# Key blocks copied out of PSUM once and masked from SBUF by VectorE, in a two-layer spectral and attention kernel

## The chip, the cores and the metric

The kernel runs on one core of a Trainium2 chip. The metric is the device time of one execution in microseconds (us). Engine names in the profile: PE is TensorE's matmuls, PEld its weight loads, DVE is VectorE, ACT is ScalarE, POOL is GpSimd, SP is SyncE, which here only issues DMAs.

## What is computed

The input x is 2048 rows of 512 bf16 values. Two different sublayers alternate, twice each:

```
x = x + A(layernorm(x)); x = x + B(layernorm(x))      # layer one
x = x + A(layernorm(x)); x = x + B(layernorm(x))      # layer two
A: irfft2(rfft2(x) * (w_r + 1j*w_i))                  # a spectral filter over rows and columns
B: q = x@wq in 32 heads of 16; k = x@wk, v = x@wv     # one key and one value head for all
   softmax(q k^T / 4) v, heads joined, @ wo
```

## The kernel before, in words

The 2048 rows are held as four blocks t of four 128-row tiles r. A program in Python (class Plan, lines 116 to 578) writes down the order of every instruction ahead of time. Each piece of work is a Task with an engine (or a choice of engines), an assumed duration, its dependencies and a place in an order of preference; Plan keeps a clock for each engine and always issues what can start first. So a change of one task's durations or dependencies, or of one of Plan's constants, changes the order of everything that is issued behind it.

Sublayer A (add_front, add_middle, add_back, lines 732 to 876) is done as matrix products with tables. Its back end goes block by block, t = 0 to 3: inverse transforms (inv, L1197, copied out at L1257), additions on VectorE (radix_v, L67 to L77), the product y that gives the new rows (y_mm, L1237), for blocks 1 to 3 the addition to x (add_x, L1248), row statistics (bn, L1028 and L1029), the reciprocal deviation on ScalarE (rstd, L1040 and L1041), a small shift (L1045), the normalisation (apply, L1052), the transposes (tr_n, L1254, copied out at L1257), and then keys, queries and values of the block.

The keys of a block are one product k_mm (L1271) into one PSUM bank. The weight wk8 repeats the 16 key columns eight times, so the 128 partitions hold eight copies of the key block, and two layouts are made of it: KA keeps the even copies and zeroes the odd, KB the reverse. The masks are the two columns of `part` (zeros and ones, one per partition). Before the change both layouts are written straight from the PSUM bank, by two tasks that may each go to ScalarE (L1277) or VectorE (L1279); the bank is released when both are done. Values are one product v_mm (L1283) and four small copies (L1291 and L1293). Queries are qt_mm (L1297).

Sublayer B's scores (L1313) go in one of two ways. A pair of 512-wide scores goes into one of two double banks sa and is turned by ScalarE with one exponential (L1318). A single score goes into one of four banks b and is turned by VectorE with a linear map to 16-bit integers (L1325), whose bits read as bf16 approximate the exponential; groups of up to four of these get two more versions with a constant added to the integers, on GpSimd (L1329) or VectorE (L1331), and the three are averaged in the products with the values (PV, L1335). Plan deals the scores out to whichever engine is free.

While the back end still runs, only ScalarE takes scores, and only for the blocks whose keys and values are there: that stretch is called the ramp here. When the values of the last block are there (v_got, line 858), VectorE takes scores too. Within the ramp, a background matmul task may be put ahead of scores that ScalarE is about to need by as much as SLIP_RAMP; afterwards SLIP = 100 holds (line 406). The fill method (line 454) adds matmuls of zeros (L1010, L1014) where TensorE would be slack. When a block of attention rows is done, its results are transposed and scaled on VectorE (L1342 to L1362), projected (proj, L1366), added to x, and for layer two the front end's work on them is mixed into layer one's attention.

SBUF tiles of the tag xnt (six buffers) hold the normalised rows that are transposed.

Of the kernel before, what the change touches and what calls it, by code (L numbers as in the profile page):

```python
# [8 lines left out]
ACT = mybir.ActivationFunctionType  # L9
ALU = mybir.AluOpType  # L10
P = 128
BF = mybir.dt.bfloat16
# [86 lines left out]
class Task:  # L99
# [5 lines left out]
    def __init__(self, eng, dur, deps, fn, take=None, give=(), then=None, prio=-1, order=0, lazy=0.0, gap=0.0, parts=1, port=False, lock=False, cols=None):  # L105
        self.ways = {eng: dur} if isinstance(eng, str) else dict(zip(eng, dur))
        self.eng, self.deps, self.fn = next(iter(self.ways)), deps, fn
        self.dur = self.ways[self.eng]
        self.take, self.give, self.then = take, give, then
        self.port, self.lock = port, lock  # L110
        self.cols = self.dur * 512.0 / 220.0 if cols is None else cols
        self.prio, self.order, self.lazy, self.gap, self.parts, self.step = prio, order, lazy, gap, parts, 0
        self.end = self.slot = None


class Plan:
# [25 lines left out]
    LATE = 0.0  # L142
    GAP = 0.0
    SLIP = 100.0
    SLIP_RAMP = 1200.0
    PATIENT = 1000.0
    URGE = 150.0
    TURN = 7000.0
# [231 lines left out]
    def pe_next(self):  # L380
# [21 lines left out]
        for b in self.bg_next("PE"):  # L402
            k, n = b[3], 99
            late = T - max(b[5], k.born)
            if kinds and c[0][0] <= b[0] + k.dur + self.PE_SW:
                room = max(limit, c[0][0]) + (self.SLIP if self.at.dve_on else self.SLIP_RAMP) - b[0] - self.PE_SW
                fit = int(room / (k.dur / k.parts)) if room > 0 else 0
# [270 lines left out]
class Layer:  # L678
# [15 lines left out]
    def __init__(self, plan, em, first, last):  # L694
        self.plan, self.em, self.first, self.last = plan, em, first, last
        self.next = None
        self.at = Attn(plan, em, self)
        self.rs = {}
        self.Pk, self.G, self.FT, self.W, self.Dz, self.IT, self.UT, self.V, self.sb, self.xn, self.xt = ({} for _ in range(11))
        self.mm1_done = {}  # L700
        self.g_done = {}
        self.stat = {}
        self.gate = []
        self.two, self.direct = ((x[0] if first else x[1]) for x in (self.TWO, self.DIRECT))
        self.sd_of = {}
# [95 lines left out]
    def add_back(self):  # L801
        p, em, at = self.plan, self.em, self.at
        left = [T]
        for t in range(T):
            o = 20 + 10 * t
            cs = []
            for b in range(2):
                es = []
                for j in range(2):
                    if t == 0 and not self.direct:  # L810
                        m = p.add("PE", 440.0, [self.mid[2 * j]], lambda k, t=t, b=b, j=j: em.inv(self, t, b, j, k.slot, (0,)),
                                  take="b", order=o)
                        n = p.add("PE", 440.0, [m, self.mid[2 * j + 1]],
                                  lambda k, t=t, b=b, j=j, m=m: em.inv(self, t, b, j, m.slot, (1,)), order=o)
                    elif t == 0:
                        m = p.add("PE", 880.0, [self.fil[2 * j]], lambda k, b=b, j=j: em.inv0(self, b, j, k.slot, 0),
                                  take="b", order=o)
                        n = p.add("PE", 880.0, [m, self.fil[2 * j + 1]],
                                  lambda k, b=b, j=j, m=m: em.inv0(self, b, j, m.slot, 1), order=o)
                    else:  # L820
# [3 lines left out]
                                    give=(m,), order=o))  # L824
# [3 lines left out]
            for j in range(0, R, w):  # L828
                key, ks = ("b", t, j), []
                for i, r in enumerate(range(j, j + w)):  # L830
# [3 lines left out]
                              order=o + 1)  # L834
                    if put:
                        c = p.add("ACT", 482.0, [y], lambda k, t=t, r=r, y=y: em.put_x(t, r, y.slot), order=o + 1)
# [7 lines left out]
                                    order=o + 2))  # L844
# [4 lines left out]
                for a in range(j, j + w, 2):  # L849
# [3 lines left out]
                                    lambda k, t=t, a=a, x=x: em.trn_evac(self, t, a, x.slot, k.eng), give=(x,), order=o + 4))  # L853

            def k_got(k, t, i):
                at.k_ready[(t, i)] = k.end + p.LAT[k.eng]
# [7 lines left out]

            m = p.add("PE", 870.0, te, lambda k, s, t=t: em.k_mm(self, t, k.slot, s), parts=4, take="b", order=o + 5)
            last = []
            for i in range(2):
                last.append(p.add(*self.flex(t, 586.0, 667.0), [m], lambda k, t=t, i=i, m=m: em.k_evac(t, i, m.slot, k.eng), order=o + 5))
            p.both(*last, m, lambda k, t=t, last=last: k_got(k, t, last.index(k)))
            if t == 0:  # L870
                at.add_qt((0, 0), te, o + 5)
            m = p.add("PE", 800.0, te, lambda k, s, t=t: em.v_mm(self, t, k.slot, s), parts=4, cols=256.0, take="b", order=o + 6)
# [52 lines left out]
class Emit:  # L925
# [345 lines left out]
        self.nc.tensor.matmul(self.ps(slot), lhsT=self.wk8[:, c, :], rhs=self.xTc(L.at, t, c), start=(c == 0), stop=(c == NC - 1),  # L1271
                              skip_group_check=True)

    def k_evac(self, t, i, slot, eng):
        out, part = (self.KA, self.KB)[i][:, 512 * t:512 * t + 512], self.part[:, i:i + 1]
        if eng == "ACT":
            self.nc.scalar.activation(out=out, in_=self.ps(slot), func=ACT.Identity, scale=part)  # L1277
        else:
            self.nc.vector.tensor_scalar(out=out, in0=self.ps(slot), scalar1=part, scalar2=None, op0=ALU.mult)  # L1279

    def v_mm(self, L, t, slot, r):
        for c in range(NC):
# [174 lines left out]
```

## Time and profile before

| what | us |
|---|---|
| median of 3 runs | 1343.77 (1343.35 to 1345.37) |
| the profiled execution | 1343.35 |
| its span, first to last instruction | 1341.6 |
| VectorE busy, ScalarE busy | 1291.2, 1225.7 |
| GpSimd busy | 849.7 |
| layer one's ramp ends (first L1325) | 110.73 |
| layer two's ramp ends (first L1325 of layer two) | 776.12 |

The granted TensorE clock is 1.00 throughout. A row of the timeline gives the start, the duration, engine, line, operation, what is written from what, the count, and in brackets the idle time of the engine just before and what ended it. Durations include an overlap with the next instruction of the same engine, so distances between starts are what an instruction costs its engine; two evacuations with 0.75 us each start 0.66 us apart, for example. Times run from the span's start.

### The profile page before, as it was taken

The page shows a single profiled execution, that of the slowest core. Times are in us where ns is not written, and L with a number is a line of the kernel's source. Part 1 is how long each engine was busy: PE and PEld are TensorE (multiplying, and loading weights), DVE is VectorE, ACT ScalarE, POOL GpSimd, SP SyncE. Part 2 cuts the span into 40 slices and gives each one's busy share as a digit, 9 for nine tenths or more (in the row PEclk, how much of TensorE's full clock was granted, in tenths as well). Part 3 has the DMA queues.
Part 4 walks back from the last instruction along what each step waited for, and adds up shares of the span by engine and source line. Part 5 has one row for each costly group of instructions (what it writes and reads, how often), then busy time and mean ns, then how long its engine had stood idle before and what let it go on. Part 6 is the DMA issues. An engine that isn't in the chain of part 4 may idle for free. (4 is left out here: it accounts for less than half of the span.)

```text
span 1341.6 us, 31639 instructions
## 1 busy us (share of the span) xinstructions
PE 1310.9 (98%) x13046; PEld 428.0 (32%) x13046; DVE 1291.2 (96%) x2317; ACT 1225.7 (91%) x1390; POOL 849.7 (63%) x831
## 2 busy tenths in 40 slices
PE   9999999999999999999999999999999999999998
PEld 4642222222222222222246422222222222322222
DVE  6998999999999999999969999999999999999998
ACT  6478999999999999899954889999999999998996
POOL 0004777767776777667720068777777777876775
PEclk9999999999999999999999999999999999999999
DMA  9100000010001000100051000000000000000000
GB/s 292 41 1 1 2 1 2 2 33 1 2 2 33 1 2 2 32 2 2 1 165 41 1 1 1 2 2 6 13 2 2 6 13 2 2 1 17 1 1 17
DMA packets 29041, 25.16 MB, mean 19 GB/s; under 512 B 8672, under 2 KB 27616, under 8 KB 28896
## 3 DMA queue, kind: packets, MB, share of 16 engines
q1 hardware_dynamic: 28608, 22.58, 5.7%
q8 instruction: 102, 1.67, 0.5%
q10 hardware_dynamic: 288, 0.56, 0.1%
q14 instruction: 43, 0.35, 0.1%
HBM read 17.89 MB, written 3.67 MB: 16 GB/s over the span
## 5 line engine op out<-in xcount | busy, mean ns | idle before, releaser
L1313 PEld LDWEIGHTS <-KB 32*128 32x128 bf16 x2048 | 83.9, 91 | 224.0 <-issue 218.5
L1313 PEld LDWEIGHTS <-KA 32*128 32x128 bf16 x2048 | 82.3, 91 | 226.0 <-issue 217.8
L1335 PEld LDWEIGHTS <-vs_108 128*32 128x32 bf16 x2464 | 96.3, 94 | 111.3 <-issue 107.7
L1335 PEld LDWEIGHTS <-vs_109 128*32 128x32 bf16 x1632 | 96.3, 94 | 71.4 <-issue 69.0
L1335 PEld LDWEIGHTS <-vs_111 128*32 128x32 bf16 x1632 | 72.1, 94 | 72.7 <-issue 67.6
L1335 PEld LDWEIGHTS <-vs_110 128*32 128x32 bf16 x1632 | 70.0, 94 | 75.4 <-issue 71.9
L1329 POOL INT64_ADD w_1384<-w_1383 x1 | 1.0, 1041 | 110.5 <-DVE w_1383 L1325 110.5
L1329 POOL INT64_ADD w_10948<-w_10947 x1 | 1.0, 1039 | 97.7 <-DVE w_10947 L1325 97.7
L1318 ACT ACTIVATE e_2_86<-sa_65 128x1024 bf16<-128x1024 f32 x47 | 51.1, 1088 | 4.5 <-PE sa_64 L1313 4.0
L1318 ACT ACTIVATE e_12_96<-sa_65 128x1024 bf16<-128x1024 f32 x47 | 51.1, 1087 | 4.5 <-PE sa_64 L1313 4.1
L1318 ACT ACTIVATE e_5_89<-sa_65 128x1024 bf16<-128x1024 f32 x49 | 53.2, 1086 | 1.8 <-PE sa_64 L1313 1.0
L1318 ACT ACTIVATE e_7_91<-sa_64 128x1024 bf16<-128x1024 f32 x50 | 54.7, 1095 | 0.0
L1318 ACT ACTIVATE e_9_93<-sa_65 128x1024 bf16<-128x1024 f32 x49 | 53.2, 1086 | 1.6 <-PE sa_64 L1313 0.8
L1318 ACT ACTIVATE e_0_84<-sa_65 128x1024 bf16<-128x1024 f32 x47 | 51.7, 1101 | 3.2 <-PE sa_64 L1313 3.1
L1318 ACT ACTIVATE e_6_90<-sa_65 128x1024 bf16<-128x1024 f32 x49 | 53.1, 1083 | 1.5 <-PE sa_64 L1313 1.0
L1318 ACT ACTIVATE e_1_85<-sa_64 128x1024 bf16<-128x1024 f32 x50 | 54.2, 1083 | 0.0
L1318 ACT ACTIVATE e_3_87<-sa_65 128x1024 bf16<-128x1024 f32 x47 | 51.4, 1093 | 2.3 <-PE sa_64 L1313 2.0
L1318 ACT ACTIVATE e_11_95<-sa_65 128x1024 bf16<-128x1024 f32 x47 | 51.4, 1093 | 2.2 <-PE sa_64 L1313 1.9
L1318 ACT ACTIVATE e_4_88<-sa_65 128x1024 bf16<-128x1024 f32 x49 | 53.0, 1081 | 0.1
L1318 ACT ACTIVATE e_12_96<-sa_64 128x1024 bf16<-128x1024 f32 x48 | 52.7, 1099 | 0.2 <-PE sa_64 L1313 0.2
L1318 ACT ACTIVATE e_10_94<-sa_64 128x1024 bf16<-128x1024 f32 x49 | 52.5, 1072 | 0.1
L1318 ACT ACTIVATE e_3_87<-sa_64 128x1024 bf16<-128x1024 f32 x48 | 52.2, 1086 | 0.1
(4003 smaller groups left out, 6246.9 us busy)
## 6 DMA issues: line engine op xcount, KB each, us to landing
it<-const_IT SPq DMA_DIRECT2D x8, 640.0 KB, 6.3
x_sb<-in_A_x_dram SPq DMA_DIRECT2D x4, 512.0 KB, 6.9
out_dram<-x_sb SPq DMA_DIRECT2D x16, 128.0 KB, 1.8
way<-x_sb SPq DMA_DIRECT2D x6, 256.0 KB, 2.2
tab_PH<-const_PH ACTq DMA_DIRECT2D x1, 512.0 KB, 5.1
w_123<-const_FT SPq DMA_DIRECT2D x1, 512.0 KB, 8.8
w_128<-const_FT SPq DMA_DIRECT2D x1, 512.0 KB, 8.5
tab_PS<-const_PS SPq DMA_DIRECT2D x1, 512.0 KB, 7.9
```

What stands on the lines that cost most here:

```text
L1313: self.nc.tensor.matmul(o, lhsT=KX[rs, kc * P:(kc + 1) * P], rhs=at.QT[qb][rs, g, :], start=True, stop=True, skip_group_check=True)
L1318: self.wrote("ACT", e, self.nc.scalar.activation(out=e, in_=self.ps(slot), func=ACT.Exp, scale=SCALE))
L1329: self.nc.gpsimd.int64_add(t[p][:, 0:n].bitcast(U64), t[0][:, 0:n].bitcast(U64), DELTA[p] * FOUR)
L1335: self.nc.tensor.matmul(self.ps(slot)[32 * h:32 * h + 32, :], lhsT=V[:, kc, :], rhs=rhs, start=first, stop=last, skip_group_check=True)
```

## The change

The product of a block's keys is copied out of PSUM once, to an SBUF tile of the tag xnt (on ScalarE or VectorE, as Plan chooses), which releases the bank; then VectorE writes KA and KB, each from that tile times a column of `part`. K8 holds the tile until both are written. SLIP_RAMP goes from 1200 to 600. Nothing else is changed; the first x of layer one was already turned by TensorE.

```
-    SLIP_RAMP = 1200.0
+    SLIP_RAMP = 600.0
...
             m = p.add("PE", 870.0, te, lambda k, s, t=t: em.k_mm(self, t, k.slot, s), parts=4, take="b", order=o + 5)
             last = []
+            c = p.add(*self.flex(t, 482.0, 600.0), [m], lambda k, t=t, m=m: em.k_evac(self, t, m.slot, k.eng), give=(m,), order=o + 5)
             for i in range(2):
-                last.append(p.add(*self.flex(t, 586.0, 667.0), [m], lambda k, t=t, i=i, m=m: em.k_evac(t, i, m.slot, k.eng), order=o + 5))
-            p.both(*last, m, lambda k, t=t, last=last: k_got(k, t, last.index(k)))
+                p.add("DVE", 323.0, [c], lambda k, t=t, i=i: em.k_part(self, t, i), then=lambda k, t=t, i=i: k_got(k, t, i), order=o + 5)
...
-    def k_evac(self, t, i, slot, eng):
-        out, part = (self.KA, self.KB)[i][:, 512 * t:512 * t + 512], self.part[:, i:i + 1]
-        if eng == "ACT":
-            self.nc.scalar.activation(out=out, in_=self.ps(slot), func=ACT.Identity, scale=part)
-        else:
-            self.nc.vector.tensor_scalar(out=out, in0=self.ps(slot), scalar1=part, scalar2=None, op0=ALU.mult)
+    def k_evac(self, L, t, slot, eng):
+        L.K8[t] = self.pool.tile([P, 512], BF, name="xnt", tag="xnt", bufs=6)
+        self.copy(eng, L.K8[t], self.ps(slot))
+
+    def k_part(self, L, t, i):
+
+        self.nc.vector.tensor_scalar(out=(self.KA, self.KB)[i][:, 512 * t:512 * t + 512], in0=L.K8[t], scalar1=self.part[:, i:i + 1],
+                                     scalar2=None, op0=ALU.mult)
```

More of the change, by code (lines that the diff above doesn't have):

```diff
@@ L698, in __init__ @@
         self.rs = {}
-        self.Pk, self.G, self.FT, self.W, self.Dz, self.IT, self.UT, self.V, self.sb, self.xn, self.xt = ({} for _ in range(11))
+        self.Pk, self.G, self.FT, self.W, self.Dz, self.IT, self.UT, self.V, self.sb, self.xn, self.xt, self.K8 = ({} for _ in range(12))
         self.mm1_done = {}
```

## The prediction

> **What bounds the kernel now.** I read the page from the top: busy shares, then the forty slices.
>
> ```profile
> PE 1310.9 (98%) x13046; PEld 428.0 (32%) x13046; DVE 1291.2 (96%) x2317; ACT 1225.7 (91%) x1390; POOL 849.7 (63%) x831
> ...
> DVE  6998999999999999999969999999999999999998
> ACT  6478999999999999899954889999999999998996
> POOL 0004777767776777667720068777777777876775
> ```
>
> VectorE (DVE) and ScalarE (ACT) are both at 9 in almost every slice of the two attention stretches. That is the plan's intention: a score pair goes to ScalarE as an exponential (starts 0.91 us apart) or its two halves go to VectorE (L1325, 0.60 us apart each), and work is dealt out so that both stay full. Holes are left at the two ramps (slices 3-4 and 22-24, the spectral back end that feeds the keys) and at the layer ends. An edit that touches only the ramp is paid in ramp time, once per layer. So next I read VectorE's timeline of layer one's ramp, at the lines with idle time (in brackets: idle before, and who ended it):
>
> ```profile
> 95.37 0.75 DVE L1279 TENSOR_SCALAR KA<-b_68,part 128x512 bf16<-128x512 f32 x1 [0.72 <-PE b_68 L1271]
> ...
> 97.04 0.69 DVE L1248 TENSOR_TENSOR x_sb<-b_67,x_sb 128x512 bf16<-128x512 f32 x1 [0.40 <-PE b_67 L1237]
> ...
> 104.54 0.16 DVE L1045 SCALAR_TENSOR_TENSOR sb<-mv,sb 128x4 f32<-128x4 f32 x1 [1.31 <-ACT sb L1041]
> ...
> 108.44 0.75 DVE L1279 TENSOR_SCALAR KA<-b_67,part 128x512 bf16<-128x512 f32 x1 [1.11 <-PE b_67 L1271]
> ...
> 110.73 0.69 DVE L1325 TENSOR_SCALAR w_1383<-b_69 128x512 uint16<-128x512 f32 x1 [1.02 <-PE sa_64 L1313]
> ```
>
> From 72 to 110.7 us VectorE is full but for these 4.56 us, so it paces the ramp, and attention at full rate begins at 110.73. The last hole comes from the key chain itself, on ScalarE and on TensorE (PE):
>
> ```profile
> 109.22 0.69 ACT L1277 ACTIVATE KB<-b_67,part 128x512 bf16<-128x512 f32 x1 [2.88 <-DVE KA L1279]
> ```
> ```profile
> 109.96 0.38 PE L1010 MATMUL b_67<-zero 128*128 128x512 bf16 x1 [0.73 <-ACT KB L1277]
> 110.27 0.39 PE L1313 MATMUL sa_65<-w_915,KA 32*128 32x512 bf16 x2
> ```
>
> The two evacuations of one bank run one after the other (KB starts 0.03 us after KA's end at 109.19), and a filler matmul into the same bank stands ahead of the scores and waits for KB. The scores need only KA, yet start at 110.27. Layer two shows the same (773.82, 774.61, 775.34, 775.65).
>
> **The change, part by part.** Sums are made against the profiled execution, 1343.35 us (span 1341.6 and 1.75 around it); the median of the runs shown is 1343.77, and I move that by the same amount.
>
> *Blocks 0 to 2, VectorE.* Before, one 128x512 evacuation each (0.66 us to the next start, 82.52 to 83.18). After, two SBUF-to-SBUF writes. None is in the trace in that form; nearest is L1052, same shape, types and scalar operands, four in 1.29 us, 0.32 each. Two are 0.65. Change: nothing. The first of them waits for the copy, which may stand behind one exponential on ScalarE (0.91), and V's copies and the next adds are queued behind it; in the new order two to eight VectorE instructions stand in front and cover that. ScalarE drops 0.59 (83.29 to 83.88) for a copy at 0.48. ScalarE has holes in the ramp, so that is worth nothing until attention. No DMA is added or moved; SP's order is the same.
>
> The Trainium skill, VectorE: DVE Perf Modes, section Rules for kernel authors, says to accept the slow rate from PSUM or to copy out first if many operations follow. By that page's cycle table a masked write from SBUF would be an estimated 0.19 us, and sixteen of them would lower my sum by 2.1 us; L1052 at 0.32 speaks against it.
>
> *Block 3, VectorE.* In the changed kernel's instruction order its copy is on VectorE too (both layers). From the same matmul end: copy 0.69 (L1257 of that form) + 0.04 (a dependent start, as bn_aggr after bn_stats) + 0.32 + 0.32 + V's four small ones 0.53 = 1.90, so VectorE is free at 110.34. KA ends at 108.44+0.73+0.41 = 109.58, scores follow by 0.05 and first results by 0.46: 110.1. The first L1325 then comes at 110.34 instead of 110.73, **-0.39**; the first exponential at 110.07 instead of 110.70. What is late next is VectorE's own queue. If the scores wait for KB as well this shrinks to -0.1.
>
> *SLIP_RAMP and the new order.* Background matmuls now may delay ScalarE's scores by 0.6 us, not 1.2. In the new order TensorE computes two of block 3's four rows (L1237) before block 2's transposes, so VectorE has adds and statistics where it had 0.72 and 0.40 of idle time. Against that, block 0's KA is third in VectorE's queue, behind two statistics (0.83 each): keys at about 73.5 against 71.9, with scores, the next query matmuls and the last quarter of a row queued behind on TensorE; some 0.5 us of slack is eaten there. Bounds 0 and -1.12; walking the order row by row I get 0.2 to 0.55 and take **-0.3**. Per layer -0.7, two layers **-1.4**.
>
> *Work dealt out anew.* Counts from the instruction orders: L1325 812 to 814 in layer one and 820 to 821 in layer two; exponentials 618 to 617 and 614 to 614. Three more at 0.60 is **+1.8** on VectorE, which is full; ScalarE's gain of 0.9 waits behind it. Filler matmuls fall by three slots of 0.22 and changes of matmul kind rise by 17 (0.10 each, 87.65 to 87.97 against 0.22 within a kind): +1.0 us on TensorE at most, whose score, PV and background slots add up to about 460 of the 569 us of layer one's attention. Hidden; +1.0 if not.
>
> *Layer ends.*
>
> ```profile
> 678.36 0.67 DVE L1325 TENSOR_SCALAR w_9806<-b_68 128x512 uint16<-128x512 f32 x1
> 681.69 0.72 DVE L1342 STREAM_TRANSPOSE raw<-b_69 128x512 f32<-128x512 f32 x1 [2.65 <-PE b_69 L1335]
> ```
>
> The last group of four needs two GpSimd additions of 1.02 after it. In the new order the last group of layer one has two members and both its phases on VectorE (L1331), and the GpSimd group before it closed 1.2 us earlier: **-1.2**. In layer two the last group has one member, and GpSimd's group closed 0.6 earlier: 1.56 after the last L1325, +0.5 to PV and transpose, 2.06 against 2.20: **-0.14**. Beside L1331 at 1331.25 GpSimd's addition took 1.52 instead of 1.04, so up to +0.5 at each end stays in the range.
>
> The Trainium skill, SBUF — State Buffer, section Terms, says VectorE and GpSimd share a port pair that one instruction holds to its end. The masked writes fall where POOL shows 0.00 us busy, so it could bite only at layer one's end, up to one addition (1.04), and my sum would then be 1343.9.
>
> Sum: -1.4 + 1.8 - 1.2 - 0.14 = -0.94. 1342.41 for the profiled execution, **1342.8 us** against the median.
>
> **Rivals.**
>
> *Slower: longer gaps between ScalarE's scores.* In the whole attention plan any shift re-deals the row closings. Before has one bad place, where thirteen projection matmuls pass with scores for VectorE only:
>
> ```profile
> 555.11 1.05 ACT L1318 ACTIVATE e_3_87<-sa_64 128x1024 bf16<-128x1024 f32 x1
> 560.19 1.02 ACT L1318 ACTIVATE e_2_86<-sa_65 128x1024 bf16<-128x1024 f32 x1 [4.03 <-PE sa_64 L1313]
> ```
>
> Adding matmul slots between ScalarE's scores along the order, layer one has four gaps over 2.2 us (2.87, 2.70, 4.11, 2.72), after it six (4.43, 2.47, 2.33, 2.83, 4.24, 4.77); layer two three, after four. A gap costs about 1.1 times its length less 1.05 and less other ScalarE work: this gives 2.1 and 3.5 where the trace shows 2.08 and 4.03. By it ScalarE idles some 6 us more in layer one and 2 in layer two; with an earlier start (0.7) and two pairs fewer (1.8) its last exponential comes 3.4 later, at 683.2; PV and transpose 1.0 behind that move the transpose from 681.69 to 684.2, +2.5; layer two adds 0.1 to 1. About **1347.0**. It decides once ScalarE's added idle time in layer one exceeds about 2.7 us: 679.84 - 2.5 + 1.0 then reaches 681.0, where VectorE's sum puts the transpose. Against it: VectorE was never starved in the 4.03 gap, and the plan, which counts those gaps, took only one exponential off ScalarE.
>
> *Nothing.* VectorE is the full engine, and the ramp's gain is eaten by its three extra L1325 and by GpSimd at the ends: -1.4 + 1.8 - 0.6, about **1343.6**.
>
> *Faster.* Both ramps give the upper bound (1.12 and 0.63, -2.1 beyond my value), and the one 1.54 us wait of L67 for GpSimd at 578.6 is missed by the new order: **1339.2**.
>
> **How the numbers follow.** Forecast 0.41, nothing 0.14, slower 0.23, faster 0.22. 0.2% is 2.7 us, about what a measurement of this kernel can tell from no change, so the lines are 1341.1 and 1346.5, and the first two cases lie between them: same 0.55. The range takes in both outer cases but for their far halves: 1339.5 to 1347.2.
>
> **What would show it.** Right: KB no longer waits for ScalarE, no PE wait on an evacuation ahead of the first block 3 scores; first L1325 near 110.0 and near 775.4 less layer one's shift; masked writes near 0.41 us, starting 0.32 apart; the transpose at layer one's end about 1.5 us after the last L1325. Wrong: ScalarE waits on sa scores adding up to 5 us more than now, or VectorE idle before the masked writes while the copy queues behind an exponential (0.91 each).

## The result, and the profile after

The changed kernel takes **1349.37 us** (median, 1349.17 to 1349.62), the kernel before 1343.56 in runs beside it: ratio 1.0041, 95% interval 1.0023 to 1.0058. It is slower by 5.8 us; the forecast was 1342.8 us, with a range that ended at 1347.2. Two profiled executions of experiments were disturbed (2531 and 5897 us instead of 1338) and their traces are not read; the medians of these two kernels are the times of undisturbed executions.

The page of the changed kernel, busy shares and two rows of slices, to be held against those in the prediction:

```profile
PE 1315.5 (98%) x13031; PEld 434.1 (32%) x13031; DVE 1295.9 (96%) x2333; ACT 1222.7 (91%) x1387; POOL 850.1 (63%) x832
...
DVE  6999999999999999999979999999999999999998
ACT  6479999998998999899954799999999999999996
```

The page shows almost nothing: VectorE is busy 4.7 us longer, ScalarE 3.0 us less, and of ScalarE's slices in layer one's attention three stand at 8 where one did. So the span has to be cut where one stage ends and the next begins: first score on VectorE (L1327, L1325 before), last transpose of the layer (L1344, L1342 before), and the same in layer two.

| stage, us | before | after | difference | forecast |
|---|---|---|---|---|
| start to layer one's first VectorE score | 110.73 | 108.93 | -1.80 | -0.7 |
| layer one's attention | 570.96 | 576.53 | **+5.57** | +0.0 (scores +1.2, end -1.2) |
| between the layers | 94.43 | 92.48 | -1.95 | -0.7 |
| layer two's attention | 557.22 | 560.83 | **+3.61** | +0.5 (score +0.6, end -0.14) |
| after it, to the end of the execution | 10.01 | 10.40 | +0.39 | 0 |

The last row's 0.39 lies outside the profiled span, which in both kernels ends 8.23 us after the last transpose.

Both ramps gained more than twice what was forecast. The whole loss, 9.2 us, is in attention, where the change does nothing but move work. The table by windows has, for each stretch, its length and then busy time and instructions of PE, PEld, DVE, ACT and POOL. Before, both attention stretches:

```profile
110.73:681.69 570.96, 562.50 (x5798) 159.66 (x5796) 563.26 (x963) 558.17 (x612) 421.73 (x412) 1.00 0.05 12
776.12:1333.34 557.22, 549.51 (x5766) 156.64 (x5765) 551.00 (x924) 544.92 (x590) 425.59 (x409) 1.00 0.01 4
```

and after:

```profile
108.93:685.46 576.53, 566.07 (x5797) 162.78 (x5797) 566.12 (x967) 556.66 (x611) 422.06 (x412) 1.00 0.04 11
777.94:1338.77 560.83, 553.10 (x5760) 159.45 (x5760) 553.32 (x927) 545.26 (x590) 425.65 (x410) 1.00 0.01 4
```

Length less busy time is idle time. In layer one ScalarE's rises from 12.79 to 19.87 and VectorE's from 7.70 to 10.41; in layer two from 12.30 to 15.57 and from 6.22 to 7.51. The busy times of the two together hardly change in layer one (1121.43 and 1122.78). Scores can go to either, so what one loses the other must take: the stretch is half of (both busy times + both idle times), and its 5.57 us are half of 1.35 more busy and 9.79 more idle. Layer two's 3.61 are half of 4.56 more idle and 2.66 more busy (1095.92 to 1098.58): part of it is one more score on VectorE, and two additions of a constant (L1333) there, 0.57 and 1.12 us, where there was one of 0.69. So by this count idle time is 7.2 of the 9.2 us, and busy time 2.0. TensorE's work is not what grew: it loads weights 5797 times in layer one's stretch, for 5796 before. VectorE's 2.71 in layer one is a difference of two things: its wait at the very end falls from 2.65 to 0.70, and its waits before that rise by 4.66.

Where ScalarE idles: its timeline at the two longest holes after the change, and TensorE's at the second of them.

```profile
314.65 1.02 ACT L1320 ACTIVATE e_9_93<-sa_65 128x1024 bf16<-128x1024 f32 x1 [4.14 <-PE sa_64 L1315]
...
563.12 1.04 ACT L1320 ACTIVATE e_12_96<-sa_64 128x1024 bf16<-128x1024 f32 x1
567.50 1.02 ACT L1320 ACTIVATE e_2_86<-sa_65 128x1024 bf16<-128x1024 f32 x1 [3.34 <-PE sa_64 L1315]
```
```profile
562.38 0.39 PE L1315 MATMUL sa_64<-w_7013,KB 32*128 32x512 bf16 x2
562.70 0.61 PE L1368 MATMUL b_69<-WO,w_6267 128*128 128x512 bf16 x2
563.14 1.03 PE L1368 MATMUL b_67<-WO,w_6267 128*128 128x512 bf16 x4
564.01 1.03 PE L1368 MATMUL b_68<-WO,w_6267 128*128 128x512 bf16 x4
564.87 1.03 PE L1299 MATMUL b_69<-gx,wq 128*128 128x512 bf16 x4
...
567.07 0.39 PE L1315 MATMUL sa_65<-w_7013,KB 32*128 32x512 bf16 x2
```

At 562.70 fourteen background matmuls (ten projections, four of a query) pass in a row, then PV products and two scores for VectorE, and ScalarE's next scores come 4.7 us after the last. (In the hole before 314.65 eight query products pass, and the next scores need the query that VectorE then copies out.) This time VectorE starves as well, in other such stretches, the longer of them thirteen first products of layer two (L1099):

```profile
449.98 0.69 DVE L1257 CAST w_4729<-b_66 128x512 bf16<-128x512 f32 x1 [2.69 <-PE b_66 L1299]
...
575.36 0.69 DVE L1327 TENSOR_SCALAR w_8213<-b_68 128x512 uint16<-128x512 f32 x1
578.99 0.69 DVE L1327 TENSOR_SCALAR w_8261<-b_67 128x512 uint16<-128x512 f32 x1 [2.94 <-PE b_68 L1315]
```
```profile
576.54 0.69 ACT L1112 ACTIVATE w_8236<-b_67,sb 128x512 bf16<-128x512 f32 x1
```

The projections' results are added to x by VectorE (L1248), which so has work while they pass; those of L1099 are copied out by ScalarE (L1112), and VectorE has none.

The ramp, VectorE's timeline at its end, where before had KA at 108.44, KB on ScalarE at 109.22 and the first score at 110.73:

```profile
107.15 0.69 DVE L1257 CAST xnt<-b_69 128x512 bf16<-128x512 f32 x1 [1.26 <-PE b_69 L1271]
107.87 0.35 DVE L1280 TENSOR_SCALAR KA<-xnt,part 128x512 bf16<-128x512 bf16 x1
108.14 0.35 DVE L1280 TENSOR_SCALAR KB<-xnt,part 128x512 bf16<-128x512 bf16 x1
...
108.93 0.68 DVE L1327 TENSOR_SCALAR w_1385<-b_66 128x512 uint16<-128x512 f32 x1
```
```profile
108.28 0.39 PE L1315 MATMUL sa_65<-w_918,KA 32*128 32x512 bf16 x2 [0.46 <-DVE KA L1280]
```

This end is as forecast: the scores wait for KA alone, no filler stands ahead waiting for KB, and VectorE's own queue is what is late. Only everything is 1.3 us earlier already when the key product ends.

### The profile page after: what moved, and what is told of

Its sections match the earlier page's. It is cut to its first block, busy times and chain, and to the rows that moved or that the text cites. A ratio compares the mean times of both kernels' runs of the same rounds, so it can differ in the third digit from the quotient of the medians.

```text
span 1347.0 us, 31631 instructions
## 1 busy us (share of the span) xinstructions
PE 1315.5 (98%) x13031; PEld 434.1 (32%) x13031; DVE 1295.9 (96%) x2333; ACT 1222.7 (91%) x1387; POOL 850.1 (63%) x832
## 4 chain that ended last, share of the span: by engine, by line
ACT 45%; PE 34%; DVE 18%; issue 2%; POOL 1%; DVEq 0%; POOLq 0%; ACTq 0%
PE sa_65 L1315 4%; PE b_67 L1337 4%; ACT e_9_93 L1320 4%; ACT e_12_96 L1320 3%; ACT e_0_84 L1320 3%; ACT e_3_87 L1320 3%; ACT e_4_88 L1320 3%; ACT e_10_94 L1320 3%; ACT e_8_92 L1320 3%; PE sa_64 L1315 3%; ACT e_7_91 L1320 3%; ACT e_2_86 L1320 3%; ACT e_1_85 L1320 3%; ACT e_11_95 L1320 3%; ACT e_5_89 L1320 3%; ACT e_6_90 L1320 3%
## 5 line engine op out<-in xcount | busy, mean ns | idle before, releaser
L1315 PEld LDWEIGHTS <-KA 32*128 32x128 bf16 x2048 | 85.2, 91 | 223.6 <-issue 212.4
L1331 POOL INT64_ADD w_1386<-w_1385 x1 | 1.0, 1041 | 109.0 <-DVE w_1385 L1327 109.0
L1331 POOL INT64_ADD w_10959<-w_10958 x1 | 1.0, 1039 | 96.8 <-DVE w_10958 L1327 96.8
```

The source lines that it names most:

```text
L1315: self.nc.tensor.matmul(o, lhsT=KX[rs, kc * P:(kc + 1) * P], rhs=at.QT[qb][rs, g, :], start=True, stop=True, skip_group_check=True)
L1331: self.nc.gpsimd.int64_add(t[p][:, 0:n].bitcast(U64), t[0][:, 0:n].bitcast(U64), DELTA[p] * FOUR)
```

## The experiments

Theory A: the new operations gain in the ramps, and the loss is the order of attention that Plan dealt anew, with longer stretches of background matmuls between scores. Theory B: the new operations cost by themselves. Each kernel is built from one of the two with the edit shown. "Ramp" in the table runs from block 0's first key evacuation to VectorE's first score, so that a shift of a few tenths in the front end is left out; idle is VectorE / ScalarE in each attention stretch. One kernel has no stages here; those of the copies on ScalarE are from a further execution of that kernel (1337.77 us).

| kernel | median us | ratio to before, 95% | ramp | L1 attention | idle | between | L2 attention | idle |
|---|---|---|---|---|---|---|---|---|
| before | 1343.56 | | 39.50 | 570.96 | 7.7 / 12.8 | 94.43 | 557.22 | 6.2 / 12.3 |
| after | 1349.37 | 1.0023-1.0058 | 37.63 | 576.53 | 10.4 / 19.9 | 92.48 | 560.83 | 7.5 / 15.6 |
| old order, new keys | 1343.56 | 0.9987-1.0004 | 39.16 | 571.17 | 7.7 / 12.9 | 94.11 | 557.78 | 6.8 / 12.6 |
| new order, old keys | 1351.98 | 1.0045-1.0070 | 38.76 | 576.73 | 10.4 / 19.8 | 93.62 | 561.01 | 7.4 / 15.5 |
| keys only | 1359.47 | 1.0104-1.0132 | 39.46 | 579.19 | 13.6 / 21.2 | 94.40 | 565.10 | 9.4 / 21.3 |
| SLIP_RAMP only | 1353.27 | 1.0056-1.0083 | 39.24 | 577.49 | 10.6 / 22.3 | 94.09 | 562.47 | 8.2 / 18.8 |
| after, SLIP 400 | **1334.98** | 0.9921-0.9946 | 37.63 | 569.42 | 7.9 / 8.7 | 92.54 | 553.84 | 3.8 / 8.8 |
| before, SLIP 400 | 1338.36 | 0.9947-0.9974 | 39.51 | 569.05 | 7.5 / 8.0 | 94.40 | 554.00 | 3.8 / 8.6 |
| after, SLIP 0 | 1374.56 | 1.0218-1.0246 | 37.63 | 587.08 | 19.5 / 33.2 | 92.53 | 574.97 | 17.1 / 35.5 |
| after, GAP 1500 | 1347.02 | 1.0015-1.0034 | 37.84 | 578.13 | 17.2 / 16.4 | 92.74 | 556.72 | 6.9 / 9.4 |
| after, SLIP 800 | 1341.99 | 0.9982-1.0000 | 37.65 | 573.19 | 10.4 / 14.0 | 92.50 | 557.04 | 4.1 / 12.9 |
| after, SLIP 400, GAP 1000 | 1341.78 | 0.9982-1.0000 | 38.31 | 574.30 | 12.6 / 13.9 | 93.29 | 557.07 | 7.1 / 10.9 |
| after, SLIP 400, SLIP_RAMP 1200 | 1338.62 | 0.9947-0.9975 | 39.46 | 569.27 | 7.5 / 8.7 | 94.39 | 553.93 | 3.6 / 9.1 |
| before, SLIP 400, SLIP_RAMP 600 | 1338.47 | 0.9946-0.9973 | | | | | | |
| after, SLIP 400, SLIP_RAMP 1200, copies on ScalarE | 1338.27 | 0.9942-0.9969 | 39.13 | 568.89 | 7.2 / 8.4 | 94.07 | 554.38 | 4.0 / 9.3 |
| after, SLIP 400, copies of blocks 1 to 3 on VectorE | 1342.96 | 0.9982-1.0000 | 39.81 | 571.80 | 13.6 / 10.7 | 94.67 | 554.87 | 3.1 / 9.5 |

**Order against operations.** The old order with the new operations in its places (k_evac is called twice per block, as before):

```
     def k_evac(self, t, i, slot, eng):
-        out, part = (self.KA, self.KB)[i][:, 512 * t:512 * t + 512], self.part[:, i:i + 1]
...
+        if t not in K8:
+            K8[t] = self.pool.tile([P, 512], BF, name="xnt", tag="xnt", bufs=6)
+            self.copy("ACT", K8[t], self.ps(slot))
+            return
+        k8 = K8.pop(t)
+        for j in range(2):
+            self.nc.vector.tensor_scalar(out=(self.KA, self.KB)[j][:, 512 * t:512 * t + 512], in0=k8, scalar1=self.part[:, j:j + 1],
+                                         scalar2=None, op0=ALU.mult)
```

> The instruction order of the kernel before, kept as it is, with the new key operations put in place of the old ones: at each block's first key task ScalarE copies the bank to SBUF, at its second VectorE writes both masked layouts from SBUF. Theory A (the loss is the re-dealt order of attention: longer stretches of background matmuls between ScalarE's scores, and ScalarE starves): attention as before, 571 us in layer one and 557 us in layer two within 1.5 us each, ScalarE's waits in them near 11 and 10 us as before, whole time 1342 to 1345.5 us. Theory B (the new operations themselves cost time, by more work on VectorE or by a port shared with GpSimd): most of the 5.8 us loss stays, 1347 us or more.

And the new order with the old operations, where k_mask is the old evacuation from PSUM, KB in the copy's place and KA in the first masked write's:

```
+    def k_evac(self, L, t, slot, eng):
+        L.K8[t] = slot
+        self.k_mask(t, 1, slot, eng)
+    def k_part(self, L, t, i):
+        if i == 0:
+            self.k_mask(t, 0, L.K8[t], "DVE")
```

> The instruction order of the changed kernel, with the old key operations in its places: the copy's place writes KB from PSUM (ScalarE or VectorE, as planned), the first masked write's place writes KA from PSUM on VectorE, the second is empty. Theory A: the loss is there although no new key operation is: attention near 576.5 and 561 us (against 571 and 557 before), ScalarE's waits near 19 and 15 us, 1348 to 1351 us whole. Theory B: about the time of the kernel before, 1342 to 1345 us. It also tells what the new operations are worth in the ramp: the first L1327-type write of layer one came at 108.93 us in the changed kernel, 110.73 before; if the operations make that gain it is near 110.7 here, if the order makes it near 109.

The windows of the new order with old keys:

```profile
110.53:687.26 576.73, 563.40 (x5771) 162.98 (x5797) 566.37 (x967) 556.91 (x611) 422.04 (x412) 1.00 0.04 11
780.88:1341.89 561.01, 551.40 (x5743) 159.87 (x5760) 553.61 (x925) 545.51 (x590) 425.65 (x410) 1.00 0.01 4
```

Without one new key operation, both attention stretches are the changed kernel's within 0.2 us, and the busy times of VectorE and ScalarE in them within 0.3. With the new operations in the old order they are the old ones within 0.6. Theory B falls. The ramp tells something else: the new order alone gains 0.74 us (39.50 to 38.76), the new operations in the old order 0.34, both together 1.87; in layer two 0.81, 0.32 and 1.95.

**Each half alone.** The changed kernel with SLIP_RAMP back, and the kernel before with SLIP_RAMP changed:

```
-    SLIP_RAMP = 600.0
+    SLIP_RAMP = 1200.0
```

> The changed key tasks with SLIP_RAMP left at 1200, order planned anew. Along its instruction order the gaps over 2.2 us between ScalarE's scores are eight in layer one (up to 4.8) and six in layer two (up to 3.7), by the gap formula of the prediction 25.5 and 17.5 us of ScalarE waits against 16.0 and 8.9 for the order before and 21.5 and 13.9 for the changed kernel's. Theory A: slower than the changed kernel or like it, 1349 to 1354 us. If SLIP_RAMP were what costs: near 1343 us.

```
-    SLIP_RAMP = 1200.0
+    SLIP_RAMP = 600.0
```

> The kernel before with SLIP_RAMP 600 alone, old key tasks, order planned anew. Gaps over 2.2 us: seven in layer one (none over 3.6), five in layer two; formula 23.4 and 13.4 us. Theory A: any re-dealing of this plan that lengthens the gaps costs, so 1347 to 1352 us without any new key operation. Theory B (key operations cost): 1343 to 1345 us. If SLIP_RAMP alone were the gain in the ramp, the first VectorE score write of layer one comes near 109.5 instead of 110.73.

Both are slower than the changed kernel, and slower than expected (1359.5 for 1349 to 1354, 1353.3 for 1347 to 1352). Either half alone costs attention more than the two together (8.2 and 7.9 us, 6.5 and 5.3, against 5.6 and 3.6), and neither has the ramp's gain.

**Is it the idle time?** The next edits change one constant of Plan, here SLIP, by which background work may delay ScalarE's scores in attention, first in the changed kernel and then in the one before. The formula of the expectations adds up ScalarE's waits from the gaps along the instruction order, as the prediction's slower rival did:

```
-    SLIP = 100.0
+    SLIP = 400.0
```

> The changed kernel with SLIP 400 for 100: a background matmul may delay the scores that ScalarE is about to need by 0.4 us, so that it passes one or two at a time and not a long stretch at once. Gaps over 2.2 us along the order: two of 2.4 in layer one, one of 3.5 in layer two; formula 8.8 and 4.4 us. The six kernels measured so far give, per microsecond of the formula's waits, 0.86 us of attention in layer one (from 571.1 at 16.0) and 0.85 in layer two (from 557.5 at 8.9). Theory A: attention near 565 and 554 us, 1330 to 1334 us whole. Rival D (what counts is how many scores VectorE gets, 0.60 us each; 1626 here, 1632 before, 1635 in the changed kernel): 5.4 us off the changed kernel at most, 1344 us or a little less. Rival E (the order scatters by causes of its own and the gaps are no more than a sign): anywhere between 1340 and 1352.

> The kernel before (old key tasks, SLIP_RAMP 1200) with SLIP 400. Formula 7.3 and 2.9 us. Theory A: attention near 563.5 and 552.5 us; with the old ramps 1329 to 1333 us, level with the changed kernel at SLIP 400 within 3 us: with the gaps gone on both sides, what is left between the two is the new keys' ramp gain (1.8 us a layer) against 1.5 us of formula in each layer. Rival D: 1626 scores on VectorE against 1632, 1340 us. Rival E: 1338 to 1352.

The changed kernel with SLIP at 0:

```
-    SLIP = 100.0
+    SLIP = 0.0
```

> The changed kernel with SLIP 0: a background matmul may not delay ScalarE's scores at all, so it waits until it is starved and then passes in a long stretch. Gaps up to 6.4 us, formula 34.7 and 29.7 us. Theory A: attention near 587 and 575 us, 1371 to 1380 us. Rival D: 1647 scores on VectorE, 12 more, 7.2 us: 1357 us. Rival E: 1340 to 1355.

And with SLIP left at 100 and GAP changed, the least distance between layer two's front-end matmuls that run inside layer one's attention:

```
-    GAP = 0.0
+    GAP = 1500.0
```

> The changed kernel with GAP 1500 for 0: matmuls of layer two's front end that run inside layer one's attention are kept 1.5 us apart. Formula 11.7 us of ScalarE waits in layer one and 0 in layer two (gaps 2.7, 3.3, 2.5, 2.5, and none). Theory A: attention near 567.5 and 550 us, 1328 to 1334 us. Rival D: 1621 scores on VectorE, 14 fewer than the changed kernel, 8.4 us: 1341 us. Rival E: 1340 to 1352.

SLIP 400 fills most of ScalarE's holes (8.7 and 8.8 us of idle time for 19.9 and 15.6). ScalarE's slices in the changed kernel with it:

```profile
ACT  6479999999999999999954799999999999999996
```

It is at 9 all through attention, both stretches shrink (553.84 in layer two as expected; 569.42 in layer one, where the line through the earlier kernels said 565), and this kernel beats both originals: 1334.98 us, 0.66% under the kernel before, and just past the 1330 to 1334 that theory A gave. The kernel before gains too, 1338.36 us, but 5 us less than theory A said (1329 to 1333), again by layer one (569.05 for 563.5). SLIP 0 is the counter-test. Its attention (587.08 and 574.97) lies where the line through the earlier kernels put it (587 and 575), and the holes stand three times in layer one, 152 us apart, each behind the projections of a finished block of attention rows:

```profile
268.10 3.77 ACT L1320 ACTIVATE e<-sa 128x1024 bf16<-128x1024 f32 x4 [6.51 <-PE sa L1315]
...
420.06 3.77 ACT L1320 ACTIVATE e<-sa 128x1024 bf16<-128x1024 f32 x4 [6.51 <-PE sa L1315]
...
572.01 3.77 ACT L1320 ACTIVATE e<-sa 128x1024 bf16<-128x1024 f32 x4 [6.51 <-PE sa L1315]
```

Rival D (the number of scores on VectorE) said 1357 there and is out by 17.6 us. The changed kernel at SLIP 400 and at 0 lies outside rival E's range too; the kernel before at SLIP 400 lies just inside it.

GAP 1500 is a miss of theory A as it was put (1347.02 us for 1328 to 1334, inside rival E's range): ScalarE idles less in both layers (16.4 for 19.9, and 9.4 for 15.6), but layer one's attention is 578.13 where the formula gave 567.5. VectorE's waits, in total, times and longest, tell why:

```profile
DVE w L1327 <- PE sa L1315: 11.2, 8, 3.6
DVE w L1327 <- PE b L1315: 4.3, 14, 0.7
```

Now scores for VectorE come late, and it idles 17.2 us. A formula that follows only ScalarE's gaps cannot see this. What holds in all the traces is the sum of both: in layer one the two engines' busy times add up to between 1121.4 and 1123.6 us in every kernel up to here, so attention changes by 0.5 us per microsecond of idle time on either. In layer two the sum is less steady, 1095.1 to 1099.5. Why Plan leaves VectorE without scores there (its PSUM banks may be held by the spaced products) was not tried.

Two more settings, chosen because the formula and the count of long gaps disagree, or because the stretches without any score are the shortest of all:

```
-    SLIP = 100.0
+    SLIP = 800.0
```

> The changed kernel with SLIP 800. No gap between ScalarE's scores is over 2.2 us, but very many are between 1.5 and 2.2: the formula, which counts all above 1.5, gives 23.3 and 14.9 us, the count of long gaps gives none. Theory A with the formula: attention near 577 and 562.5 us, 1349 to 1352 us. Rival F (only long gaps starve ScalarE, short ones are covered by the two score buffers): attention at 569 and 554 us or less, 1333 to 1336 us.

```
-    GAP = 0.0
-    SLIP = 100.0
+    GAP = 1000.0
+    SLIP = 400.0
```

> The changed kernel with SLIP 400 and GAP 1000: layer two's front-end matmuls 1 us apart as well. Formula 8.8 and 4.9 us, one gap of 2.4; stretches of matmuls without any score add up to less than in any other (2.4 us above 1.2 each in layer one, against 4.5 at SLIP 400 alone). If those stretches are what is left at SLIP 400: attention near 567.5 and 553.5, 1332 to 1334 us. If keeping the front end apart starves VectorE, as with GAP 1500 (VectorE idle 17.2 us of 578.1 in layer one although the formula gave 11.7): 1340 us or more.

Both end between the theories or against the hopeful one. SLIP 800 gives 573.2 and 557.0: many short delays do cost, but less than the formula says. GAP 1000 starves VectorE again (12.6 us). So the order's numbers tell the direction, and not the microsecond; the idle times in the trace tell it.

**Whose is the ramp's gain?** At SLIP 400 attention is alike in the three corners that have a trace (569.1 to 569.4 and 553.8 to 554.0 us), and the four corners of the change can be compared. The two that are missing set SLIP_RAMP, the first in the changed kernel at SLIP 400, the second in the one before at SLIP 400:

```
-    SLIP_RAMP = 600.0
+    SLIP_RAMP = 1200.0
```

> The new key tasks with SLIP 400 and SLIP_RAMP back at 1200: with the attention order alike on both sides (formula 7.9 and 3.5 us; 8.8 and 4.4 with SLIP_RAMP 600), it tells whose the 1.8 us per ramp are. So far the first score write of VectorE came at 108.9 to 109.3 with new keys and SLIP_RAMP 600 together, at 110.5 to 110.9 with either alone. Theory G (the gain needs both: shorter key work on VectorE only pays when the background matmuls ahead of it are not late, or the other way round): first write near 110.9, from layer one's last transpose to layer two's first write near 94.4 (92.5 with both), attention as at SLIP 400 with both (569.4 and 553.8), 1338 to 1339.5 us. Rival H (the keys alone make it, and the 110.9 of the keys-only kernel was its own order): near 1335 us, first write near 109.

```
-    SLIP_RAMP = 1200.0
+    SLIP_RAMP = 600.0
```

> The old key tasks with SLIP 400 and SLIP_RAMP 600, the fourth corner. Formula 8.0 and 3.6 us. Theory G: first write of VectorE near 110.6, between the layers near 94.1, attention near 569 and 554 us, 1337 to 1339 us. If SLIP_RAMP alone makes the ramp's gain: near 1335 us and first write near 109.2.

Old keys 1338.36 (1200) and 1338.47 (600), new keys 1338.62 (1200) and 1334.98 (600). Neither half is worth anything alone; together they take 3.4 us, nearly all of it in the two ramps. In the traces, the new keys with SLIP_RAMP 600 have three of the four copies of a layer on ScalarE, with 1200 only one. So the copies' engine was bound, first to ScalarE for blocks 0 to 2 at 1200, then to VectorE for blocks 1 to 3 at 600:

```
-            c = p.add(*self.flex(t, 482.0, 600.0), [m], ...
+            c = p.add(*(("ACT", 482.0) if t < 3 else ("DVE", 600.0)), [m], ...
```

> New key tasks, SLIP 400, SLIP_RAMP 1200, but the copies of blocks 0 to 2 bound to ScalarE and block 3's to VectorE, as the plan itself places them with SLIP_RAMP 600 (left free with 1200 it puts only block 0's on ScalarE). Attention's order is the same as with the copies free (formula 7.9 and 3.5 us). Theory G1 (SLIP_RAMP matters because it moves the copies of blocks 1 and 2 off VectorE; each is 0.72 us to the next start, two per layer): from block 0's first key evacuation to VectorE's first score write 38.0 us instead of 39.46, between the layers 93.0 instead of 94.39, whole 1335 to 1336.5 us. Theory G2 (it matters through the order of the background matmuls): 39.5, 94.4 and 1338 to 1339 us.

> The kernel of the copies bound to ScalarE at SLIP_RAMP 1200 once more, for its profile alone, since it came at 1338.3 us and so against theory G1. Theory G2 (the order of the background matmuls): the copies of blocks 0 to 2 are on ScalarE, and VectorE's 1.4 us per layer are eaten by added idle time ahead of rows that TensorE delivers late (idle time of VectorE from 70 us to its first score write 4 us or more, against 2.97 with SLIP_RAMP 600); first key evacuation to first score write 39.2 us or more. If VectorE's idle time is near 3 us and the ramp is 38 us, then the loss lies in attention and not in the ramp.

```
-            c = p.add(*self.flex(t, 482.0, 600.0), [m], ...
+            c = p.add(*(("ACT", 482.0) if t < 1 else ("DVE", 600.0)), [m], ...
```

> The other way round: new key tasks, SLIP 400, SLIP_RAMP 600, with the copies of blocks 1 to 3 bound to VectorE. Formula 6.4 and 3.8 us. Theory G1: the ramps grow by two copies at 0.72 each, from 37.63 to 39.1 us and between the layers from 92.54 to 94.0, whole 1337.5 to 1339 us. Theory G2: ramps as with the copies on ScalarE, 1334 to 1336 us.

Copies on ScalarE do not bring the gain back at 1200: the ramp is 39.13 us where theory G1 said 38.0, and the whole time 1338.27, as theory G2 said. Copies on VectorE lose it at 600 (39.81 for 37.63), by more than G1 said (39.1), and the whole time, 1342.96 us, is outside both theories: attention was dealt anew too, 2.4 and 1.0 us longer. So the copies on ScalarE are not enough; that they are needed rests on this last kernel and on the one with GAP 1000, which has two of four copies on ScalarE and a ramp of 38.31. What else it takes is to be seen in VectorE's holes in the ramp with copies on ScalarE at 1200:

```profile
95.51 0.23 DVE L1293 CAST vs<-b 128x64 bf16<-128x64 f32 x1 [1.10 <-PE b L1285]
...
96.80 0.69 DVE L1248 TENSOR_TENSOR x_sb<-b,x_sb 128x512 bf16<-128x512 f32 x1 [0.15 <-PE b L1237]
```
```profile
104.31 0.16 DVE L1045 SCALAR_TENSOR_TENSOR sb<-mv,sb 128x4 f32<-128x4 f32 x1 [1.30 <-ACT sb L1041]
...
108.20 0.69 DVE L1257 CAST xnt<-b 128x512 bf16<-128x512 f32 x1 [1.11 <-PE b L1271]
...
110.41 0.69 DVE L1327 TENSOR_SCALAR w<-b 128x512 uint16<-128x512 f32 x1 [0.34 <-PE b L1315]
```

They add up to 4.00 us, against 2.97 with SLIP_RAMP 600, where the same stretch holds two additions of block 3 ahead of block 2's copies:

```profile
93.89 1.28 DVE L1248 TENSOR_TENSOR x_sb<-b,x_sb 128x512 bf16<-128x512 f32 x2
95.09 1.27 DVE L1257 COPY gx<-b 128x1024 bf16<-128x1024 bf16 x2
```

VectorE's work became less, and VectorE waited for the next rows; with SLIP_RAMP 600 TensorE has delivered two of them by then. The holes are 1.03 of the 1.50 us between these two ramps; the rest was not taken apart.

## Why the prediction was wrong, point by point

- **Failed: "Work dealt out anew".** It counted instructions, three more scores at 0.60, +1.8 us, "on VectorE, which is full". With the ends (-1.34) the prediction had +0.5 for attention; it was +9.2. The count came true (814 and 821 scores on VectorE). What it had put at nothing is the idle time that the new order brings to both engines: 9.8 us more in layer one and 4.6 in layer two, each microsecond worth half a microsecond of time, 7.2 of the 9.2 us; busy time added the other 2.0.
- **The slower rival (chance 0.23) was the right mechanism at too small a price.** It forecast 6 and 2 us more idle time on ScalarE; the windows show 7.1 and 3.3. But it turned 6 us into 2.5 by following ScalarE's last exponential alone, less 0.7 for the earlier start and 1.8 for two pairs moved to VectorE, as if VectorE took those at no cost to the end. It argued against itself that "VectorE was never starved in the 4.03 gap". That holds for this gap of the kernel before, but not for the changed kernel: VectorE waits 2.94 us at 578.99 and 2.69 at 449.98, and idles 2.7 us more in all of layer one. Scores move between the engines, so one engine's idle time is shared, not hidden behind the other.
- **The ramps, -1.4 forecast, -3.75 measured.** The new order alone was put at -0.3 per layer and gave -0.74 and -0.81. The operations were put at -0.39 and gave -0.34 and -0.32 in the old order, but -1.13 and -1.14 in the new one. "Nothing" for blocks 0 to 2 was wrong: in both orders the two writes start 0.24 to 0.27 us apart (0.32 was taken from L1052), and the pair takes 0.50 to 0.53 to the next row where one write from PSUM took 0.66. By the cycle table of the Trainium skill, VectorE: DVE Perf Modes, section The TRN2 errata, the estimate was 0.19; start to start, the trace lies between the two. In the changed kernel's trace most of layer one's gain is fewer waits: VectorE's holes in the ramp are 2.97 us instead of 4.56.
- **Block 3's chain: right in kind.** KB no longer waits for ScalarE, the scores wait for KA alone, and the masked writes take 0.35 us. From the copy to the first score it took 1.78 us where the sum had 1.90, and the key product's end was 1.3 us earlier than the sum assumed, so the first score came at 108.93 and not 110.34.
- **Layer ends, -1.2 and -0.14 forecast.** From the last score's start to the transpose: 3.33 to 2.92 in layer one (-0.41), 2.88 to 3.30 in layer two (+0.42). GpSimd's last addition did end as much earlier after the last score as forecast (2.83 to 1.61 us, 2.38 to 2.26), but VectorE's own additions were now last. At layer one's end there are two equal ones (L1333), beside GpSimd's:

```profile
683.34 1.09 DVE L1333 TENSOR_SCALAR w_9843<-w_9842 128x1024 uint16<-128x1024 uint16 x1
684.35 0.41 DVE L1333 TENSOR_SCALAR w_9844<-w_9842 128x1024 uint16<-128x1024 uint16 x1
```
```profile
683.11 1.04 POOL L1331 INT64_ADD w_9801<-w_9799  x1
```

The first lies beside GpSimd's addition and takes 1.09 us, the second has no such neighbour and takes 0.41. The second ends at 684.76, where two of 0.41 would have ended with GpSimd's, at 684.15: an estimated 0.6 us of the end. In layer two VectorE's second addition takes 1.12 us and ends 0.14 behind GpSimd's, and from there to the transpose it is 0.90 us where it was 0.50. The prediction had left up to 0.5 for this at each end in the range, named 1.04 as the most at layer one's end, and put nothing in the sum.

## What to carry to other kernels

Where work can go to either of two engines, price a new order by the idle time of both: cut the trace into stages and take length less busy time, because each idle microsecond on either costs half a microsecond as long as their busy times together stay the same, and a page that shows 9 in nearly every slice hid ten of them here. A planner that deals an order greedily answers any edit with a new deal, so test the edit in the old order and the old operations in the new one before it is judged; here the same edit lost 5.8 us with SLIP at 100 and gained 3.4 with SLIP at 400. Two halves of a change may each be worth nothing and together 3.4 us; here, as far as the traces show, one takes work off VectorE and the other brings its inputs early enough for it to use the time.

## What the runs showed of the hardware

- Where one of VectorE's additions (L1333, L1331 before) overlaps one of GpSimd's, the one that started second is stretched in the rows here. VectorE was second in the 128x1024 row above, which ends 0.28 us after GpSimd's addition, and at layer two's end, where a 128x512 one took 1.12 us (1336.75 to 1337.87) while GpSimd's (1336.66, 1.07 us) ended at 1337.73. The Trainium skill, SBUF — State Buffer, section Terms, says that the port pair which the two share is held for the full instruction and the loser blocks; these rows agree. In the kernel before VectorE was first (1331.25) and not stretched, 0.69 us, and GpSimd's addition, from 1331.32, took 1.52 for 1.04.
- The masked write of 128x512 bf16 from SBUF to SBUF with a column as scalar: 0.32 to 0.35 us in the changed kernel's trace, 0.24 to 0.27 from start to start.
